# A retention stage in chunks of 64 positions, by quadrants of the matmul array

## The chip, the core and the metric

One core of a Trainium2 chip runs the whole program. Its engines have their own instruction queues, each worked off in order: TensorE (PE; its weight loads are listed as PEld), VectorE (DVE), ScalarE (ACT), GpSimd (POOL) and SyncE (SP, which issues most DMAs). The metric is the device time of one execution in microseconds (us).

## The reference

Inputs are q, k and v of 4 sequences, 8 heads, 576 positions and 64 columns a head, in fp32, and the weights of two feed-forward layers. The part that matters here is the first:

```python
scores = scale * np.matmul(q, k.transpose(0, 1, 3, 2))
Dmat = np.where(rel >= 0, gamma[:, None, None] ** rel[None, :, :], 0.0)   # rel = row - column
ret = scores * Dmat[None, :, :, :]
return np.matmul(ret, v)
```

The result, with heads side by side (2304 tokens, 512 columns), goes through `h * tanh(softplus(h))` with h = x @ w_in (2048 wide) and @ w_out, and then through a gated layer of 1536 columns and its output product.

## The kernel before, in words

The decay gamma ** (row - column) is split into a factor on v (`gv`), a factor on the result (`gout`) and a causal mask. So a sequence can be worked in chunks: inside a chunk the masked scores times v, and for all earlier positions one 64x64 state a head, the running sum of k times v.

`retention` goes through 20 steps t, five a sequence: four chunks of 128 positions and a last one of 64 (numbered sc = 0 to 4; steps 4, 9, 14 and 19 have 64). Heads are held in four pairs, a pair's two heads in the two halves of the 128 partitions. A step does, in this program order, which is the order of each engine's queue (the schedule is manual):

- `scores(t)`: for each head, keys (transposed, `kT`) against queries (`qT`), K = 64, into two PSUM tiles; then two mask multiplies on DVE into `p`, one for each half of the heads (L449).
- at steps 9, 11, 14 and 17, `g1`: the first four hidden products of the next stage (L613).
- `transposes(t + 1)`: keys of the next step through PE into `tk`, copied to `kT` by ACT; POOL makes `vs`, v times its factor.
- `q_ahead`: query transposes for later steps through the one PSUM tile `tq`, each copied by two ACT copies (L395), for the last chunk by one small copy.
- ACT and POOL split a finished weight unit into two parts (`part`, L133, L134); DVE starts on another (`begin`, L119).
- `output(t)`: the product of queries with the state, all of K = 128 against a block-diagonal `sbd` (L507); `state(t)`: k times v added to a PSUM tile (L483); `state_out`: two ACT copies of it into `sbd`, read in the next step (L497); the masked scores times v on top of the state's product (L516); and the eviction with `gout` on DVE (L529).
- the end of the step: `join` (L123), `rebias` of the next weight unit on ACT and DVE (L114, L115; the first to wait for that unit's DMA), a split of finished outputs (L318, L323), `mish` and its cast for the product of the step before (L664, L671), and the loads of later q, k, v and of a weight unit (512 KB) on SP. Steps 9, 14, 18 and 19 do no weight conversion.

fp32 matmuls go through the array in two passes, so a trace counts two a product. PSUM has eight banks: the retention uses six, `pha` two that stay for the later stages. After the retention the rest of the kernel runs: the hidden products and `acc` products in turn (L613, L647), then the same layers in a scheme of seven products for eight (L842), whose tiles alternate between the two banks of `pha`.

Of the kernel before, what the change touches and what calls it, by code (L numbers as in the profile page):

```python
# [16 lines left out]
def retention_mish_swiglu(  # L17
# [27 lines left out]
    LAG = 4  # L45
    NA = 18
# [16 lines left out]
    pha = ctx.enter_context(tc.tile_pool(name="pha", bufs=2, space=PSUM))  # L63
# [272 lines left out]
    def retention(g1, mish, g_hi, g_lo):  # L336
        with ExitStack() as c0:
# [7 lines left out]
            mask = cp.tile([128, 128], F32, tag="mask", name="mask")  # L345
            gv = cp.tile([128, nsc, H], F32, tag="gv", name="gv")
            gout = cp.tile([128, NP, nsc * 128], F32, tag="gout", name="gout")
            gstep = cp.tile([128, NP, nsc], F32, tag="gstep", name="gstep")
            sbd = cp.tile([128, NP, 128], F32, tag="sbd", name="sbd")
# [17 lines left out]
            def load(t, nm, src):  # L367
                if 0 <= t < len(steps):
                    b, sc, n = steps[t]
                    x = ld.tile([128, H, D], F32, tag=nm, name=f"{nm}{t}", bufs=4 if nm == "k" else 3)  # L370
                    nc.sync.dma_start(
                        out=x[:n], in_=src[b, :, sc * 128:sc * 128 + n, :].rearrange("h p d -> p h d")
                    )
                    qkv[nm, t] = x
# [42 lines left out]
            def transposes(t):  # L417
# [9 lines left out]
                vs[t] = at.tile([128, H, D], F32, tag="vs", name=f"vs{t}")  # L427
                nc.gpsimd.tensor_tensor(
# [5 lines left out]

            def scores(t):
                b, sc, n = steps[t]
                s = [ps1.tile([128, NP, 128], F32, tag=f"s{e}", name=f"s{e}_{t}") for e in range(2)]
                for pr in range(NP):
                    for e in range(2):
                        nc.tensor.matmul(  # L440
                            s[e][:n, pr, :n],
                            lhsT=kT[t][64 * e:64 * e + 64, pr, :n],
                            rhs=q_cols(t)[64 * e:64 * e + 64, pr],
                            start=True,
                            stop=True,
                        )
                pp[t] = [at.tile([128, NP, 128], F32, tag=f"p{e}", name=f"p{e}_{t}") for e in range(2)]
                for e in range(2):
                    nc.vector.tensor_tensor(  # L449
                        out=pp[t][e][:n, :, :n],  # L450
                        in0=s[e][:n, :, :n],
                        in1=mask[:n, :n].unsqueeze(1).to_broadcast([n, NP, n]),
                        op=ALU.mult,
                    )
# [19 lines left out]
            def state(t):  # L474
# [3 lines left out]
                if sc == 0:  # L478
                    stp[b] = ps1.tile([128, NP, D], F32, tag="st", name=f"state{b}")
                for pr in range(NP):  # L480
                    for e in range(2):
# [3 lines left out]
                            lhsT=qkv["k", t][:n, h, :],  # L485
                            rhs=vs[t][:n, h, :],
                            start=(sc == 0 and pr == 0),
                            stop=(sc == nsc - 2),
                            skip_group_check=True,
                        )  # L490

            def state_out(t):
                b, sc, n = steps[t]
                if sc == nsc - 1:
                    return
                for e in range(2):
                    nc.scalar.copy(  # L497
                        out=sbd[64 * e:64 * e + 64, :, 64 * e:64 * e + 64],
                        in_=stp[b][64 * e:64 * e + 64, :, :],
                    )  # L500

            def output(t):
                b, sc, n = steps[t]
                o = ps1.tile([128, NP, 128], F32, tag="o", name=f"o{t}")
                if sc:
                    for pr in range(NP):
                        nc.tensor.matmul(  # L507
                            o[:, pr, :n], lhsT=sbd[:, pr, :], rhs=q_cols(t)[:, pr],
                            start=(pr == 0), stop=False, skip_group_check=True,
                        )  # L510
                q_ahead(t, 1)
                state(t)
                state_out(t)
                for pr in range(NP):
                    for e in range(2):
                        nc.tensor.matmul(  # L516
                            o[64 * e:64 * e + 64, pr, :n],
                            lhsT=vs[t][:n, 2 * pr + e, :],
                            rhs=pp[t][e][:n, pr, :n],
                            start=(sc == 0 and pr == 0), stop=True, skip_group_check=True,  # L520
                        )
                t0 = b * S + sc * 128
                done = 0
                while done < n:
                    j, off = divmod(t0 + done, T)
                    m = min(n - done, T - off)
                    if j not in xt:
                        new_x(xt, j, "x")
                    nc.vector.tensor_tensor(  # L529
                        out=xt[j][:, :, off:off + m],  # L530
# [658 lines left out]
```

## Time and profile before

| | us |
|---|---|
| median of 3 runs | 916.92 (916.43 to 917.99) |
| profiled execution | 916.83 |
| its span, first to last instruction | 915.0 |
| PE busy | 904.5 |
| DVE busy | 565.7 |
| ACT busy | 378.2 |
| first product after the retention starts at | 105.67 |

The span is what the trace covers; the execution's own time is 1.8 us longer. Busy time of PE contains the time in which matmuls wait in the pipeline, so 99% does not mean that PE could do no more. The granted TensorE clock is 1.00 over the span. The stage that the change touches is the first 105.67 us.

### The profile page before, as it was taken

What the parts mean: (1) busy time and instruction counts of PE and PEld (TensorE: products, weight loads), DVE (VectorE), ACT (ScalarE), POOL (GpSimd) and SP (SyncE); (2) the same over time, 40 slices, a digit from 0 to 9 for tenths busy, and PEclk for the clock granted to TensorE, in tenths of its full rate; (3) what the DMA queues carried; (4) which work ended last, traced back from release to release, by engine and by line L of the source; (5) the groups of instructions that cost most, each with busy time, mean ns of one, the idle gap of its engine ahead of it and who ended that gap; (6) DMA issues with size and microseconds to landing.
All of it is one profiled execution on the core that took longest, in us unless ns stands there. A gap on an engine that the chain in (4) does not pass through costs nothing.

```text
span 915.0 us, 15212 instructions
## 1 busy us (share of the span) xinstructions
PE 904.5 (99%) x5828; PEld 861.5 (94%) x5828; DVE 565.7 (62%) x1094; ACT 378.2 (41%) x790; POOL 57.0 (6%) x55
## 2 busy tenths in 40 slices
PE   8999999999999999999999999999999999999998
PEld 7888999999999999999999999999999999999997
DVE  3888598467767864677664666747444556444444
ACT  3867466445555544444444333323222223222222
POOL 3654200000000000000000000000000000000000
PEclk9999999999999999999999999999999999999999
DMA  9999265257886647598737566545544444644421
GB/s 219 255 242 250 70 185 184 81 191 270 273 276 210 226 166 266 175 309 284 240 119 299 198 199 198 177 161 182 198 161 161 161 161 160 216 158 160 159 93 69
DMA packets 125016, 177.58 MB, mean 194 GB/s; under 512 B 46352, under 2 KB 83984, under 8 KB 124944
## 3 DMA queue, kind: packets, MB, share of 16 engines
q1 hardware_dynamic: 123840, 176.19, 60.9%
q8 instruction: 46, 0.75, 0.3%
q10 hardware_dynamic: 1104, 0.42, 0.2%
q14 instruction: 26, 0.21, 0.1%
HBM read 133.07 MB, written 43.52 MB: 193 GB/s over the span
## 4 chain that ended last, share of the span: by engine, by line
PE 90%; DVE 4%; DMA 2%; ACT 2%; issue 1%; SPq 0%; ACTq 0%; DVEq 0%
PE t L842 28%; PE fa L1022 16%; PE h L613 14%; PE acc L647 13%; PE ea L884 7%; PE te L842 6%; PE o L516 2%; DMA q<-in_q_dram 1%; DMA raw<-in_moe_w_out_dram 1%; PE s L440 1%; PE acc L855 1%; PE o L507 1%; DVE p L449 1%; DVE raw L123 1%; PE tk L424 0%
## 5 line engine op out<-in xcount | busy, mean ns | idle before, releaser
L842 PE MATMUL t<-y,su 128*128 128x384 f32 x1512 | 306.7, 338 | 1.1 <-ACT p L1094 0.6
L842 PEld LDWEIGHTS t<-y,su 128*128 128x128 f32 x1512 | 270.7, 188 | 24.5 <-DVE cv L849 1.8
L1022 PE MATMUL fa<-fu,g 128*128 128x512 f32 x648 | 190.2, 395 | 0.1
L613 PE MATMUL h<-xs,u 128*128 128x384 f32 x768 | 143.7, 336 | 0.0
L647 PE MATMUL acc<-g,u 128*128 128x384 f32 x720 | 134.6, 335 | 0.4 <-DVE u L134 0.4
L613 PEld LDWEIGHTS h<-xs,u 128*128 128x128 f32 x768 | 133.9, 188 | 0.4
L647 PEld LDWEIGHTS acc<-g,u 128*128 128x128 f32 x720 | 125.8, 188 | 0.7 <-DVE u L134 0.7
L1022 PEld LDWEIGHTS fa<-fu,g 128*128 128x128 f32 x648 | 118.5, 188 | 7.7 <-ACT g L1045 0.5
L1045 ACT CAST g<-sg 128x384 fp32r<-128x384 f32 x72 | 37.0, 513 | 173.3 <-DVE sg L1081 120.5
L884 PE MATMUL ea<-ge,u 128*128 128x256 f32 x576 | 77.3, 281 | 0.0
L884 PEld LDWEIGHTS ea<-ge,u 128*128 128x128 f32 x576 | 75.4, 189 | 0.0
L675 DVE TENSOR_TENSOR g<-m,g 128x384 fp32r<-128x384 f32 x64 | 36.6, 571 | 60.2 <-ACT g L671 58.8
L842 PE MATMUL te<-ye,eu 128*128 128x384 f32 x336 | 67.9, 337 | 0.0
L1070 ACT ACTIVATE sg<-sg 128x384 f32<-128x384 f32 x54 | 28.4, 526 | 91.2 <-DVE sg L849 91.2
L1050 DVE TENSOR_TENSOR g<-sg,g 128x384 fp32r<-128x384 f32 x72 | 40.2, 558 | 40.7 <-ACT g L1045 40.7
L664 ACT ACTIVATE m<-h 128x384 f32<-128x384 f32 x64 | 31.2, 488 | 66.1 <-PE h L613 66.1
L842 PEld LDWEIGHTS te<-ye,eu 128*128 128x128 f32 x336 | 56.9, 188 | 0.0
L849 DVE TENSOR_TENSOR u<-t,p 128x384 f32<-128x384 f32 x36 | 20.0, 556 | 44.3 <-PE t L842 41.1
L849 DVE TENSOR_TENSOR v<-t,p 128x384 f32<-128x384 f32 x36 | 20.0, 556 | 35.4 <-PE t L842 34.7
L671 ACT CAST g<-m 128x384 fp32r<-128x384 f32 x64 | 32.9, 514 | 1.8
L1081 DVE TENSOR_TENSOR sg<-sg,cv 128x384 f32<-128x384 f32 x54 | 30.2, 558 | 1.9
L123 DVE SCALAR_TENSOR_TENSOR raw<-raw 128x512 uint32<-128x512 uint32 x32 | 28.4, 886 | 0.0
(117 smaller groups left out, 963.7 us busy)
## 6 DMA issues: line engine op xcount, KB each, us to landing
su<-comb SPq DMA_DIRECT2D x126, 512.0 KB, 3.3
comb<-c SPq DMA_DIRECT2D x84, 256.0 KB, 2.6
eu<-ecomb SPq DMA_DIRECT2D x28, 512.0 KB, 4.9
raw<-in_moe_w_in_dram SPq DMA_DIRECT2D x16, 512.0 KB, 5.5
raw<-in_moe_w_out_dram SPq DMA_DIRECT2D x16, 512.0 KB, 3.9
ecomb<-e_s SPq DMA_DIRECT2D x32, 256.0 KB, 2.3
rawg<-in_moe_w_gate_dram SPq DMA_DIRECT2D x12, 512.0 KB, 5.6
ecomb<-u SPq DMA_DIRECT2D x24, 256.0 KB, 3.2
```

Of the source, the lines that this page charges most:

```text
L123: nc.vector.scalar_tensor_tensor(lo, hi, 3, lo, op0=ALU.logical_shift_left, op1=ALU.bitwise_or)
L613: nc.tensor.matmul(ps, lhsT=u[:, a, kk * 128:(kk + 1) * 128], rhs=s[:, e, :], start=(c == 0), stop=(c == n - 1),)
L647: nc.tensor.matmul(accs[b][d][:, :T], lhsT=u[:, a, d * 128:(d + 1) * 128], rhs=g[:, e, :], start=(i == 0 and c == 0), stop=(i == F1 - 1 an ...
L664: nc.scalar.activation(w, hs.pop(s), AF.Mish)
L671: nc.scalar.copy(out=gs[s][:, 0, :], in_=ws[s])
L675: nc.vector.tensor_tensor(out=g[:, 1, :], in0=ws.pop(s), in1=g[:, 0, :].bitcast(F32), op=ALU.subtract)
L842: nc.tensor.matmul(p, lhsT=w[:, a, kk * 128:(kk + 1) * 128], rhs=y[kk][:, x, :], start=begin and kk == 0 and (a, x) == (0, 0), stop=kk == ...
L849: nc.vector.tensor_tensor(out=out_, in0=a, in1=b_, op=ALU.add)
L884: nc.tensor.matmul(o, lhsT=u[:, a, d * 128:(d + 1) * 128], rhs=y, start=f == 0 and (a, x) == (0, 0) and (r == 0 or r == 2 and d % 2 == 0), ...
L1022: nc.tensor.matmul(accs["f", b][m], lhsT=gs[u, e, h][:, x, m * 128:(m + 1) * 128], rhs=fu[2 * (u % PAIRS) + e][:, a, :], start=first, stop ...
L1045: nc.scalar.copy(out=gs[u, e, h][:, 0, :], in_=x)
L1050: nc.vector.tensor_tensor(out=g[:, 1, :], in0=x, in1=g[:, 0, :].bitcast(F32), op=ALU.subtract)
```

## The change

Everything in the retention goes by chunks of C = 64 positions, two to a step. The scores of a step become four blocks (two chunks, two heads of a pair) in the four 64x64 quadrants of the array, into one tile `s` of two banks, with one mask multiply; the cross terms between a step's two chunks go through the state. The state is updated twice a step, each time from half of the positions, and each time ACT copies it whole into a fresh `sbd` tile (three buffers). The product with the state is done for each chunk, each head by itself on the diagonal quadrants, into two PSUM tiles `o0` and `o1`; the product with v uses four quadrants; two evictions follow. The last chunk puts the two heads of a pair into the two halves of the partitions, for which v is loaded by two DMAs and its factor `gvl` by two more.

The order of a step is new: first state update, `part`, `begin` and `join`, `mish` and its cast, product with the state, key transposes, query transposes, `g1`, second state update, scores of the next step, product with v, masks of the next step, and the end of the step as before. Query transposes and query loads come one step earlier. `pha` keeps one bank; `phb` takes another after the retention, and `front` alternates between them.

```diff
-    pha = ctx.enter_context(tc.tile_pool(name="pha", bufs=2, space=PSUM))
+    pha = ctx.enter_context(tc.tile_pool(name="pha", bufs=1, space=PSUM))
...
+                    if n == C and nm == "v":
+                        for e in range(2):
+                            nc.sync.dma_start(
+                                out=x[C * e:C * e + C, :NP, :],
+                                in_=src[b, :, sc * 128:sc * 128 + n, :].rearrange("(a e) p d -> e p a d", e=2)[e],
+                            )
+                        return
...
                 due = (
-                    ((b, 1, 0),) if b else (),
-                    ((b, 1, 1),) if b else ((b, 1, 0), (b, 1, 1)),
-                    ((b, 2, 0),),
-                    ((b + 1, 0, 0),),
+                    ((b, 1, 1),) if b else (),
+                    ((b, 2, 0),) if b else ((b, 1, 0), (b, 1, 1)),
+                    ((b + 1, 0, 0),) if b else ((b, 2, 0), (b + 1, 0, 0)),
                     ((b + 1, 0, 1),),
+                    ((b + 1, 1, 0),),
                 )[sc]
...
             def scores(t):
...
+                for pr in range(NP):
+                    for c in range(n // C):
+                        for e in range(2):
+                            nc.tensor.matmul(
+                                s[C * c:C * c + C, e, pr, :],
+                                lhsT=kT[t][64 * e:64 * e + 64, pr, C * c:C * c + C],
+                                rhs=q_cols(t)[64 * e:64 * e + 64, pr, C * c:C * c + C],
+                                start=True,
+                                stop=True,
+                            )
+
+            def masks(t):
...
+                nc.vector.tensor_tensor(
+                    out=pp[t][:, :r], in0=s[:, :r],
+                    in1=mask.unsqueeze(1).unsqueeze(1).to_broadcast([128, r, NP, C]),
+                    op=ALU.mult,
+                )
...
-            def state(t):
+            def state(t, c):
...
-                            lhsT=qkv["k", t][:n, h, :],
-                            rhs=vs[t][:n, h, :],
+                            lhsT=qkv["k", t][C * c:C * c + C, h, :],
+                            rhs=vs[t][C * c:C * c + C, h, :],
...
+                sbd[t, c] = at.tile([128, NP, D], F32, tag="sbd", name=f"sbd{t}_{c}", bufs=3)
+                nc.scalar.copy(out=sbd[t, c], in_=stp[b])
+
+            def inter(t):
...
+                                outs_[t][c][64 * e:64 * e + 64, pr, :],
+                                lhsT=sbd[(t, 0) if c else (t - 1, 1)][64 * e:64 * e + 64, pr, :],
+                                rhs=q_cols(t)[64 * e:64 * e + 64, pr, C * c:C * c + C],
...
+            def products(t):
...
+                                o[c][64 * e:64 * e + 64, pr, :],
+                                lhsT=vs[t][C * e:C * e + C, pr, :] if n == C else vs[t][C * c:C * c + C, 2 * pr + e, :],
+                                rhs=pp[t][C * e:C * e + C, 0, pr, :] if n == C else pp[t][C * c:C * c + C, e, pr, :],
...
+            for e in range(2):
+                nc.scalar.dma_start(
+                    out=gvl[C * e:C * e + C], in_=gv_d[:C, nsc - 1, :].rearrange("p (a e) -> e p a", e=2)[e]
+                )
...
+            scores(0)
+            masks(0)
             for t in range(len(steps)):
-                scores(t)
-                if t in EARLY:
-                    g1(EARLY.index(t))
-                transposes(t + 1)
-                q_ahead(t, 0)
+                state(t, 0)
                 while stage[3] < stage[2]:
                     part(NA)
                 x = due.pop(0) if due else None
                 conv = t not in REST
                 on = conv and begin()
-                if t + 1 < nsc:
-                    gout_chunk(t + 1)
-                output(t)
                 if on:
                     join(stage[2])
                     stage[2] += 1
+                if t - 1 in EARLY:
+                    mish(EARLY.index(t - 1))
+                    g_hi(EARLY.index(t - 1))
+                inter(t)
+                transposes(t + 1)
+                q_ahead(t, 0)
+                if t in EARLY:
+                    g1(EARLY.index(t))
+                state(t, 1)
+                q_ahead(t, 1)
+                if t + 1 < nsc:
+                    gout_chunk(t + 1)
+                scores(t + 1)
+                products(t)
+                masks(t + 1)
...
                 if t == 0:
                     load_q(4)
-                load_q(t + 5)
+                    load_q(5)
+                load_q(t + 6)
...
+            return front(name) if n >= LAG else pha.tile([128, T], F32, tag="h", name=name)
+
+        nfront = [0]
+
+        def front(name):
+            nfront[0] += 1
+            return (pha, pools["phb"])[nfront[0] % 2].tile([128, T], F32, tag="h", name=name)
...
+        pools["phb"] = ctx.enter_context(tc.tile_pool(name="phb", bufs=1, space=PSUM, reuse_waits="tile"))
...
-                    t[tn] = pha.tile([128, T], F32, tag="h", name=f"te{i}_{tn}")
+                    t[tn] = front(f"te{i}_{tn}")
```

## Rows read from the trace of the kernel before

**Rows 1.** The page: busy us of each engine (share of the span) and instructions.
```profile
PE 904.5 (99%) x5828; PEld 861.5 (94%) x5828; DVE 565.7 (62%) x1094; ACT 378.2 (41%) x790; POOL 57.0 (6%) x55
```

**Rows 2.** Timeline of PE, 0 to 110: start, length in us, instructions, [idle before].
```profile
15.52 0.66 PE L393 MATMUL tq<-ident,q 128*128 128x128 f32 x4 [0.80 <-DMA q<-in_q_dram]
...
17.62 0.66 PE L393 MATMUL tq<-ident,q 128*128 128x128 f32 x4 [0.55 <-DVE qT L395]
...
19.70 1.18 PE L440 MATMUL s<-qT,kT 64*128 64x128 f32 x16
...
57.07 1.27 PE L440 MATMUL s<-qT,kT 64*128 64x128 f32 x16
...
105.67 2.35 PE L613 MATMUL h<-xs,u 128*128 128x384 f32 x12
```

**Rows 3.** Windows: length; busy us (instructions) by engine; granted clock; DMA share; GB/s.
```profile
25.00:50.00 25.00, 24.16 (x338) 21.23 (x335) 23.27 (x34) 18.73 (x37) 16.51 (x14) 1.00 1.10 255
...
75.00:100.00 25.00, 24.57 (x313) 21.80 (x313) 18.45 (x29) 16.28 (x31) 11.11 (x9) 1.00 0.77 184
...
125.00:150.00 25.00, 25.00 (x146) 25.00 (x145) 22.61 (x42) 17.31 (x32) 0.00 (x0) 1.00 0.60 188
```

**Rows 4.** Timeline of PE in step 6.
```profile
37.08 1.16 PE L440 MATMUL s<-qT,kT 64*128 64x128 f32 x16
38.17 0.66 PE L424 MATMUL tk<-ident,k 128*128 128x128 f32 x4
...
39.10 1.06 PE L507 MATMUL o<-qT,sbd 128*128 128x128 f32 x8
40.09 0.69 PE L483 MATMUL state<-vs,k 128*64 128x64 f32 x16
40.60 1.05 PE L516 MATMUL o<-p,vs 128*64 128x128 f32 x16
41.58 1.16 PE L440 MATMUL s<-qT,kT 64*128 64x128 f32 x16
```

**Rows 5.** Timeline of PE in step 4, which has 64 positions.
```profile
28.67 0.68 PE L440 MATMUL s<-qT,kT 64*64 64x64 f32 x16
29.28 0.66 PE L424 MATMUL tk<-ident,k 128*128 128x128 f32 x4
```

**Rows 6.** Windows of 20 ns in a state update: PE busy (matmuls under way).
```profile
27.32:27.34 0.02, 0.02 (x4) 1.00 0.98 243
27.34:27.36 0.02, 0.02 (x6) 1.00 1.38 333
```

**Rows 7.** Groups by shape, 0 to 110: busy us, mean ns, idle before.
```profile
L449 DVE TENSOR_TENSOR p<-s,mask 128x512 f32<-128x512 f32 x32 | 20.5, 681 | 3.5 <-PE s L440 3.5
...
L529 DVE TENSOR_TENSOR x<-o,gout 128x256 f32<-128x256 f32 x8 | 3.2, 420 | 4.3 <-PE o L516 4.2
...
L664 ACT ACTIVATE m<-h 128x384 f32<-128x384 f32 x5 | 2.5, 491 | 4.4 <-PE h L613 4.4
...
L426 ACT COPY kT<-tk 128x256 f32<-128x256 f32 x4 | 1.5, 372 | 1.5 <-PE tk L424 1.3
```

**Rows 8.** Timeline of ACT in steps 5 and 6.
```profile
34.45 0.59 ACT L426 COPY kT<-tk 128x512 f32<-128x512 f32 x1
34.93 1.27 ACT L395 COPY qT<-tq 64x512 f32<-64x512 f32 x2
36.10 0.67 ACT L133 CAST u<-raw 128x512 fp32r<-128x512 f32 x1
...
38.17 0.70 ACT L114 ACTIVATE raw<-raw 128x512 f32<-128x512 f32 x1 [0.62 <-DMA raw<-in_moe_w_in_dram]
38.77 0.50 ACT L318 CAST xs<-x 128x384 fp32r<-128x384 f32 x1
```

**Rows 9.** The chain of waits in step 7: start, length, what.
```profile
42.49 6.58 DMA raw<-in_moe_w_out_dram
```

**Rows 10.** DMA queues, 0 to 110: packets, MB, share of 16 engines.
```profile
q1 hardware_dynamic: 54608, 23.07, 90.9%
```

More of the change, by code (lines that the diff above doesn't have):

```diff
@@ L433, in transposes @@
                 )
+            sc_ = {}
             def scores(t):
+                if t >= len(steps):
+                    return
                 b, sc, n = steps[t]
-                s = [ps1.tile([128, NP, 128], F32, tag=f"s{e}", name=f"s{e}_{t}") for e in range(2)]
-                for pr in range(NP):
[L439 to L454, printed above, removed]
+                s = ps1.tile([128, 2, 512], F32, tag="s", name=f"s{t}")[:, :, :NP * C]
@@ L489, in state @@
                             skip_group_check=True,
                         )
-            def state_out(t):
+                sbd[t, c] = at.tile([128, NP, D], F32, tag="sbd", name=f"sbd{t}_{c}", bufs=3)
+                nc.scalar.copy(out=sbd[t, c], in_=stp[b])
+            outs_ = {}
+            def inter(t):
                 b, sc, n = steps[t]
[L494 to L500, printed above, removed]
@@ L502, in output @@
-            def output(t):
-                b, sc, n = steps[t]
[L504 to L513, printed above, removed]
-                for pr in range(NP):
[L515 to L526, printed above, removed]
+                outs_[t] = [ps1.tile([128, NP, C], F32, tag=f"o{c}", name=f"o{t}_{c}") for c in range(n // C)]
@@ new lines, in inter @@
+                for c in range(n // C):
+                    for pr in range(NP if sc or c else 0):
+                        for e in range(2):
+                            nc.tensor.matmul(
+                                outs_[t][c][64 * e:64 * e + 64, pr, :],
+                                lhsT=sbd[(t, 0) if c else (t - 1, 1)][64 * e:64 * e + 64, pr, :],
+                                rhs=q_cols(t)[64 * e:64 * e + 64, pr, C * c:C * c + C],
+                                start=(pr == 0), stop=False, skip_group_check=True,
+                            )
@@ new lines, in products @@
+            def products(t):
+                b, sc, n = steps[t]
+                o = outs_.pop(t)
+                for pr in range(NP):
+                    for c in range(n // C):
+                        for e in range(2):
+                            nc.tensor.matmul(
+                                o[c][64 * e:64 * e + 64, pr, :],
+                                lhsT=vs[t][C * e:C * e + C, pr, :] if n == C else vs[t][C * c:C * c + C, 2 * pr + e, :],
+                                rhs=pp[t][C * e:C * e + C, 0, pr, :] if n == C else pp[t][C * c:C * c + C, e, pr, :],
+                                start=(sc == 0 and c == 0 and pr == 0), stop=True, skip_group_check=True,
+                            )
+                for c in range(n // C):
+                    j, off = divmod(b * S + sc * 128 + C * c, T)
@@ L544, in retention @@
             load(0, "v", v)
-            nc.scalar.dma_start(out=mask, in_=mask_d)
+            for c in range(2):
+                nc.scalar.dma_start(out=mask[C * c:C * c + C], in_=mask_d[C * c:C * c + C, C * c:C * c + C])
             nc.scalar.dma_start(out=gv, in_=gv_d)
@@ L548, in retention @@
             nc.scalar.dma_start(out=gstep, in_=gstep_d)
+            for e in range(2):
+                nc.scalar.dma_start(
+                    out=gvl[C * e:C * e + C], in_=gv_d[:C, nsc - 1, :].rearrange("p (a e) -> e p a", e=2)[e]
+                )
             load(1, "k", k)
```

62 lines of the change are left out of this document (42 added, 20 removed).

## The prediction

> **What bounds the kernel now.** The page's first part comes first: PE is busy 904.5 of 915.0 us [rows 1], so time can only leave where PE has less to do or waits less. The change touches only the retention, which ends where the first product of the next stage starts, at 105.67 [rows 2]. From 125 to 150 PE is busy 25.00 of 25 us [rows 3], and what is converted there hangs on PE's own progress. So I pass on one for one what the retention gains or loses.
>
> Inside the retention the windows show two limits close together [rows 3]: from 25 to 50 PE is busy 24.16, DVE 23.27 and ACT 18.73 of 25 us, with the DMA engines never empty (share 1.10); from 75 to 100 PE is as busy, but the DMA share is down to 0.77. One step in time order, step 6 [rows 4]: scores 37.08, transposes 38.17, product with the state 39.10, state update 40.09, product with v 40.60, next scores 41.58. That is 4.50 us without a gap: PE bounds the step.
>
> **The change, part by part.**
>
> Matmuls. A state update is 16 matmuls (eight fp32 products in two passes each) of 64 columns in two halves of the array; it takes 0.51 [rows 4], and such a group followed by another partition of the array takes 0.61 [rows 5]. I take 0.5 for a group and 0.1 for a change of partition. From one slice of 20 ns to the next the matmuls under way go from 4 to 6 [rows 6]: two start at once, and the halves run side by side. After the change a full step has the state update twice (each with half the rows, 0.5 + 0.6 for 0.51), the product with the state in two halves of two quadrants (1.0 for 0.99), and scores and product with v as 32 matmuls in four quadrants. No row shows four quadrants. If four run side by side, 32 matmuls take 0.5; if only two do, 1.0 (twice 0.51). I take 0.5, because halves by rows and halves by columns both pair in the rows. PE's step: 0.5 + 1.0 + 0.1 + 0.93 (transposes) + 0.6 + 0.5 + 0.5 = 4.1, against 4.50. Over 16 full steps that is 6.4 us off PE; the four steps of 64 positions use two quadrants before and after, and change by nothing.
>
> DVE. One mask multiply of 0.68 in place of two, and two evictions of 0.42 in place of one as wide as a mask multiply [rows 7]: 0.5 a step less, on an engine whose masks now have a whole step. Its remaining place on the path is an eviction ahead of the next product with the state; the 0.5 state update hides all but 0.2 of it. If that cover goes, 0.4 a step.
>
> The new wait. Before, a state copy had until the next step. Now the second half of a step's product with the state waits for ACT's copy of the state just made, and the next step's first state update writes the PSUM tile that ACT's second copy reads. ACT works in order, so whatever stands ahead of those copies is on the path. Going round from the start of the first copy: copy 0.37 [rows 7] and 0.06 for the signal, half product 0.5, change 0.1, transposes to their last result 0.66 [rows 4], so ACT's copy of the keys starts at 1.69. It takes 0.48 and the two query copies 1.17, by start to start [rows 8], so the second state copy starts at 3.34 and ends at 3.71. Then the next step's state update with its tail, 0.69 [rows 4], and a signal: 4.5. With the two ACT pieces of the conversion behind it, 0.60 and 0.50 [rows 8], ACT itself is ready only at 4.8. So PE's 4.1 is not reached in a step with two query copies: it takes 4.5 to 4.8, the 4.50 of before. Only the third step of each sequence, which has one small query copy, comes down to 4.1. Queued behind these copies on ACT: key copy, Mish, conversion; PE waits for the first, DVE for the last. The Mish of an early product and its cast (0.5 each [rows 7]) now stand ahead of the key copy, beside the transposes: 0.25 of them sticks out.
>
> Loads. Query tiles are loaded a step earlier, so 512 KB goes ahead of keys and of a weight unit in a queue that is always full: at 255 GB/s [rows 3] the unit lands 2.1 us later. Weight units already land when ACT wants them: one has 6.58 us of the chain [rows 9]. As such a wait now holds the next state copy, I put 0.7 on each of two steps. The last step's gate values come as 512 pieces of 4 bytes; a packet of the big queue costs 0.909 x 110 x 16 / 54608 = 29 ns of an engine [rows 10], so 0.9 us if a piece costs a packet, 0 if it hides; I keep 0.3. The split last v loads move the same bytes.
>
> The start. Step 1 transposes two groups of queries through one PSUM tile: the first at 15.52, after 0.80 of idle time for its DMA, the second at 17.62, after its copies, and scores 2 follow at 19.70 [rows 2]. In the new order these transposes have a state update (0.5), a product with the state (1.0) and a state copy with tail and signal (0.7) more ahead of them, and a change of partition (0.1). The idle 0.8 takes part of that; 1.5 is left, and it goes through to scores 2 at 21.2.
>
> Sum. Scores now stand at the end of the step before, so I compare the state's start after with the scores' end before: 22.3 for 20.8 at step 2, 1.5 late. Steps 2 to 9 by the lengths above (4.9 with two query groups; 4.5; 3.5 for 64 positions without a state copy; 4.6; 4.1 and 0.7; 4.7; 4.4 and 0.7; 5.6 with a product of the next stage) make 37.7; before 57.07 + 1.09 - 20.8 = 37.4: 1.8 late. Steps 10 to 19: 4.75, 6.15, 4.75, 4.5, 4.9, 4.75, 4.1, 5.9, 3.5, 1.2, together 44.5. Where a product of the next stage stands in a step I added 2.1 to 2.2 (12 such matmuls take 2.35 with their tail [rows 2]); steps with a Mish have 4.75, step 16 one small copy; step 19 has only its two products. Before: 105.67 - 57.07 - 1.09 = 47.5. So 3.0 is won there, and the retention ends at 104.5, 1.2 earlier. The profiled execution took 916.83 (span 915.0 and 1.8 around it; the runs' median is 916.92), so 915.6.
>
> **The rivals.**
>
> A. PE's saving comes through: ACT's copies are quicker in line than I put them, because Mish, conversion and query copies fall into gaps. For it: ACT is busy only 18.73 of 25 us. Against: the round is made of latencies, not of ACT's load. Then full steps of the second half take 4.1 to 4.2: its sum is 40.5, and half of the first half's lag is made good: 47.5 - 40.5 - 0.9 = 6 us, 910.8.
>
> B. Slower: ACT's wait for weight units. Place: the conversion's first ACT piece at the end of steps 4 to 8. Price: every landing that is 2.1 later, and 0.9 more for the small pieces, now holds a state copy and with it PE. It decides as soon as the units land later than the end of their step, which in the chain they already do [rows 9]. Four such steps at 1.1 instead of two at 0.7, and 0.9 at the start, bring 3.9 us more, so 919.5.
>
> C. Slower: the four quadrants go two at a time. Scores and product take 1.0 each; the round is then PE's 5.1, less the slack to 4.5: 0.6 in some 14 steps, 8 us more than my sum, so 924. Against: both kinds of halves pair. Beside it stands a sentence of the Trainium skill, "TensorE: Matmul & The Clock Gate", section "Wait — 56ns, not 53.3ns?": it says that matmuls never start closer together than about 25 ns. By that rule 32 matmuls take at least 0.8 us, 0.3 more than I put, twice a step; as an estimate from that page some 2 to 3 us on my sum. The trace does not agree: two matmuls start within one slice of 20 ns [rows 6].
>
> D. The 0.4 of an eviction ahead of the product with the state also sticks out: 16 x 0.2 = 3.2 us, which turns 915.6 into 918.8. I count it with B.
>
> **How the numbers follow.** A difference under 0.2%, 1.8 us, is about what a measurement of this kernel can tell from no change. My forecast, the round through ACT at about the length of PE's old step, has 0.50 and its own range is 913 to 918: of it 0.18 is faster, 0.30 within the bound, 0.02 slower. A has 0.18, all faster. B with D has 0.22: 0.10 within, 0.12 slower. C has 0.10, all slower. That makes 0.36 faster, 0.40 the same, 0.24 slower. The range goes from A's time to just past B's: 910.8 to 920.5; below it lies about 0.08, above it 0.12, most of that C.
>
> **What would show it.** Right: in the PE rows of steps 5 to 8 and 12 to 13, a group of 32 scores takes 0.5 to 0.6; the second half of the product with the state starts right after ACT's state copy, and the step is 4.5 to 4.8; the wait named on PE is ACT's, no longer DVE's mask. The first product of the next stage starts near 104.5. Wrong: 32 matmuls in 0.8 to 1.0 (C); steps of 4.1 with ACT idle ahead of each state copy (A); ACT's weight-unit wait over 3 us in steps 4 to 8 followed by PE (B). If the stage after the retention shows new gaps, passing the gain on one for one was wrong.

## The result, and where the time went

The changed kernel takes 924.08 us (median of 4 runs, 923.54 to 924.46); the kernel before took 917.17 in the same session (916.43 to 917.99). The ratio is 1.0075, with a 95% interval of 1.0057 to 1.0092: slower, and outside the range forecast. The profiled execution took 924.46, its span is 922.6, against 916.83 and 915.0.

The page first. Busy time of PE went down, not up, though it issues 1152 more instructions:

```profile
PE 900.7 (98%) x6980; PEld 858.3 (93%) x6980; DVE 555.7 (60%) x1088; ACT 376.5 (41%) x790; POOL 59.3 (6%) x55
```

DVE lost 10.0 and PE 3.8 us of busy time against [rows 1], and the span is 7.6 longer. So the loss is idle time of PE. The timeline of PE says where (start, length, instructions, idle time before and what ended it):

```profile
10.35 0.68 PE L523 MATMUL state<-vs,k 64*64 64x64 f32 x16 [0.66 <-POOL vs L446]
11.50 1.12 PE L542 MATMUL o<-qT,sbd 64*64 64x64 f32 x16 [0.47 <-ACT sbd L532]
...
19.98 0.66 PE L403 MATMUL tq<-ident,q 128*128 128x128 f32 x4 [0.92 <-DVE qT L405]
...
22.06 1.02 PE L476 MATMUL s<-qT,kT 64*64 64x64 f32 x27 [1.16 <-DVE qT L405]
...
23.62 0.31 PE L523 MATMUL state<-vs,k 64*64 64x64 f32 x1
...
28.20 0.69 PE L476 MATMUL s<-qT,kT 64*64 64x64 f32 x32
28.72 0.65 PE L555 MATMUL o<-p,vs 64*64 64x64 f32 x32
29.18 0.64 PE L523 MATMUL state<-vs,k 64*64 64x64 f32 x16
...
34.40 0.76 PE L542 MATMUL o<-qT,sbd 64*64 64x64 f32 x16 [0.60 <-DVE x L565]
...
39.33 0.68 PE L523 MATMUL state<-vs,k 64*64 64x64 f32 x16 [1.70 <-POOL vs L446]
40.54 0.68 PE L542 MATMUL o<-qT,sbd 64*64 64x64 f32 x16 [0.53 <-ACT sbd L532]
...
44.33 0.59 PE L523 MATMUL state<-vs,k 64*64 64x64 f32 x13 [0.54 <-ACT sbd L532]
...
65.09 0.27 PE L523 MATMUL state<-vs,k 64*64 64x64 f32 x1
...
113.26 2.37 PE L660 MATMUL h<-xs,u 128*128 128x384 f32 x12
```

Read it in three parts. The last line answers to 105.67 in [rows 2]: the retention ends 7.59 later, and the span is longer by 7.6, so the rest of the kernel carries that one for one. The three lines at 28 to 29 us show the quadrants doing what was hoped: 32 scores in 0.52, 32 products in 0.46 (start to start), where 16 matmuls in two halves took 0.98 to 1.09 [rows 4]. And the brackets from 34 to 45 us, two steps, name DVE, POOL and twice ACT: it is not one engine that is late. (23.62 and 65.09 are the first state updates of steps 2 and 10; they are used below.)

The windows give the account (length; busy us of PE, PEld, DVE, ACT, POOL; granted clock; DMA share; GB/s). First the kernel before, from 8 us to the end of its retention, then the changed one in the same bounds, in a stretch that answers to [rows 3], and in two short ones:

```profile
8.00:105.67 97.67, 94.06 (x1234) 82.81 (x1233) 74.98 (x109) 64.23 (x124) 50.62 (x43) 1.00 0.98 227
```

```profile
8.00:113.26 105.26, 89.77 (x2376) 79.14 (x2374) 64.09 (x102) 61.12 (x124) 53.13 (x43) 0.97 0.91 212
...
25.00:50.00 25.00, 20.59 (x587) 17.75 (x587) 17.00 (x27) 17.26 (x35) 15.66 (x14) 1.00 1.06 247
...
11.50:15.00 3.50, 3.50 (x58) 3.05 (x62) 0.00 (x0) 0.82 (x2) 2.05 (x2) 0.51 1.26 258
21.80:25.20 3.40, 3.14 (x88) 3.15 (x90) 1.27 (x4) 0.23 (x1) 0.98 (x1) 0.50 1.17 269
```

Idle time is length less busy time: 97.67 - 94.06 = 3.6 before, 105.26 - 89.77 = 15.5 after. The two short stretches ran at half clock (0.51 and 0.50, that is 1.2 GHz); of their 6.6 us of work half, 3.3, would not have been there at 2.4 GHz. The profiled execution before has no such stretch. So TensorE's work, counted at full clock, fell from 94.1 to 89.77 - 3.3 = 86.5 us, and the balance is -7.6 of work, +11.9 of idle time, +3.3 of half clock: +7.6.

Who ended the idle time stands in the waits view (engine, line, waited for: us in total, times, longest). Before:

```profile
PE o L516 <- DVE p L449: 1.7, 7, 0.6
PE tq L393 <- DMA q<-in_q_dram: 0.8, 1, 0.8
PE tq L393 <- DVE qT L395: 0.6, 1, 0.6
PE o L507 <- DVE x L529: 0.3, 1, 0.3
```

After:

```profile
PE o L542 <- DVE x L565: 2.7, 4, 1.0
PE state L523 <- POOL vs L446: 2.7, 3, 1.7
PE o L542 <- ACT sbd L532: 2.1, 4, 0.5
PE state L523 <- ACT sbd L532: 1.9, 4, 0.5
PE s L476 <- DVE qT L405: 1.2, 1, 1.2
PE tk L434 <- DMA k<-in_k_dram: 0.9, 1, 0.9
PE tq L403 <- DVE qT L405: 0.9, 1, 0.9
PE s L476 <- ACT kT L436: 0.9, 2, 0.6
PE state L523 <- issue: 0.8, 2, 0.6
PE o L555 <- issue: 0.6, 1, 0.6
```

No row holds a fifth of the 15.5. The mask, the one regular wait before, is gone; ten others came.

### The profile page after: what moved, and what is told of

It is laid out like the page before. It is cut to its first block, busy times and chain, and to the rows that moved or that the text cites. A ratio compares the mean times of both kernels' runs of the same rounds, so it can differ in the third digit from the quotient of the medians.

```text
span 922.6 us, 17529 instructions
## 1 busy us (share of the span) xinstructions
PE 900.7 (98%) x6980; PEld 858.3 (93%) x6980; DVE 555.7 (60%) x1088; ACT 376.5 (41%) x790; POOL 59.3 (6%) x55
## 4 chain that ended last, share of the span: by engine, by line
PE 90%; DVE 3%; ACT 2%; DMA 2%; POOL 1%; issue 1%; SPq 0%; ACTq 0%; POOLq 0%; DVEq 0%
PE t L898 28%; PE fa L1078 16%; PE h L660 14%; PE acc L702 13%; PE ea L940 7%; PE te L898 6%; PE o L542 1%; PE state L523 1%; DMA v<-in_v_dram 1%; PE acc L911 1%; PE tk L434 1%; PE o L555 1%; PE s L476 1%; PE tq L403 1%; DVE raw L120 1%
## 5 line engine op out<-in xcount | busy, mean ns | idle before, releaser
L730 DVE TENSOR_TENSOR g<-m,g 128x384 fp32r<-128x384 f32 x64 | 35.8, 559 | 55.5 <-ACT g L726 55.3
L565 DVE TENSOR_TENSOR x<-o,gout 128x256 f32<-128x256 f32 x36 | 13.8, 419 | 34.8 <-PE o L555 34.8
```

The lines of the kernel that those rows point to most:

```text
L730: nc.vector.tensor_tensor(out=g[:, 1, :], in0=ws.pop(s), in1=g[:, 0, :].bitcast(F32), op=ALU.subtract)
```

## The experiments

The theory at the start: the loss is a sum of single waits in the new round, above all ACT's two state copies, and each comes back when its cause is taken away. Its rival: another wait is found behind each. All times beside the runs are from their profiled executions, by the account above (end of the retention; idle time of PE from 8 us on; work at half clock; work of PE counted at full clock). Ratios are to the kernel before on the same chip.

| run | median us | ratio (95%) | end | idle | at half clock | work |
|---|---|---|---|---|---|---|
| before | 917.17 | | 105.67 | 3.6 | 0 | 94.1 |
| after | 924.08 | 1.0075 (1.0057 to 1.0092) | 113.26 | 15.5 | 6.6 | 86.5 |
| e1, new order with chunks of 128 | 933.96 | 1.0188 (1.0162 to 1.0214) | 124.75 | 17.5 | 8.9 | 94.8 |
| e2, 40 fillers | 928.04 | 1.0125 (1.0101 to 1.0149) | 117.20 | 10.9 | 3.4 | 96.6 |
| e3, no wait for the copy inside a step | 923.49 | 1.0073 (1.0057 to 1.0090) | 114.11 | 15.0 | 10.2 | 86.0 |
| e5, POOL's values first | 924.46 | 1.0083 (1.0058 to 1.0108) | 111.70 | 14.7 | 6.7 | 85.6 |
| e6, state product later in end steps | 923.33 | 1.0072 (1.0055 to 1.0090) | 115.00 | 14.6 | 10.2 | 87.3 |
| e7, second update earlier | 926.30 | 1.0105 (1.0087 to 1.0124) | 115.60 | 13.8 | 6.8 | 90.4 |
| e8, 15 fillers | 926.30 | 1.0093 (1.0076 to 1.0109) | 114.57 | 13.3 | 3.2 | 91.7 |
| e9, another bank for the queries | 926.05 | 1.0097 (1.0081 to 1.0113) | 116.10 | 15.8 | 12.9 | 85.9 |
| e10, second copy on DVE | 923.88 | 1.0079 (1.0064 to 1.0095) | 114.13 | 13.9 | 13.1 | 85.7 |
| e12, e5, e6, e10 and five key buffers | 927.52 | 1.0116 (1.0100 to 1.0133) | 116.16 | 13.6 | 17.0 | 86.0 |
| e11, before with split matmuls | 928.08 | 1.0122 (1.0107 to 1.0137) | 117.13 | 1.6 | 6.8 | 104.2 |
| x1, before with quadrant scores | 916.61 | 0.9993 (0.9984 to 1.0002) | 105.98 | 4.5 | 0 | 93.5 |
| x2, x1 and quadrant state product | 918.56 | 1.0018 (1.0008 to 1.0027) | 106.95 | 5.2 | 0 | 93.8 |
| y1, before with less of the product | 915.51 | 0.9986 (0.9977 to 0.9995) | 103.40 | 4.3 | 0 | 91.1 |

### Order or chunks (e1)

The chunking is undone, and the order, the query schedule and the loads of the change stay. The one state update of a step stands where the changed kernel has its second. Part of the edit, against the kernel before:

```diff
-                output(t)
...
+                inter(t)
+                transposes(t + 1)
+                q_ahead(t, 0)
...
+                state(t)
+                state_out(t)
+                q_ahead(t, 1)
...
+                scores(t + 1)
+                products(t)
+                masks(t + 1)
```

> Chunks of 128 positions as before, with the changed kernel's order of steps, its query schedule and its loads: only the chunking is undone. One state update and one state copy a step, scores and product as 16 matmuls in two halves. Theory 'chunks' (the second state copy a step and the half product that waits for it cost the time, and the new order is harmless): between 915 and 918, steps 10 to 19 in about 47. Rival 'order' (two query groups transposed late in step 1, scores at the end of the step, loads one step earlier cost it): 922 or more, with the second step's state update again near 23 us instead of near 20.8.

Measured: 933.96, worse than the change itself. Two steps of its PE timeline:

```profile
58.43 1.09 PE L529 MATMUL o<-p,vs 128*64 128x128 f32 x16
60.41 1.13 PE L519 MATMUL o<-qT,sbd 128*128 128x128 f32 x8 [0.89 <-DVE x L542]
...
63.67 1.09 PE L529 MATMUL o<-p,vs 128*64 128x128 f32 x16
65.65 0.52 PE L519 MATMUL o<-qT,sbd 128*128 128x64 f32 x3 [0.89 <-DVE x L542]
```

With scores at the end of a step, the product with v is followed at once by the next product with the state, which needs the same PSUM tile evicted: 0.86 to 0.95 in fourteen of the twenty steps, 12.6 us in all. The waits view up to 120 us has thirteen of them:

```profile
PE o L519 <- DVE x L542: 11.7, 13, 1.0
```

So this order without the chunks loses 17 us, and the chunks win 10 of them back. Part of that is that their first state update lies over the eviction, whose row is 2.7 in the changed kernel. The rival had the direction, and scores at the end of the step among its reasons, but not this wait. The run shows that the order costs much where nothing covers the eviction. It does not show that the order is the loss of the changed kernel, where this wait is mostly covered. The fourth kernel, chunks of 64 in the old order, was not tried.

### One wait at a time (e3, e5, e6, e7, e9, e10)

```diff
 # e3, inter(): the second half reads the copy of the step before
-lhsT=sbd[(t, 0) if c else (t - 1, 1)]...
+lhsT=sbd[(t - 1, 1) if sc else (t, 0)]...
 # e5, POOL's subtract of part() moved behind vs of the next step
                 while stage[3] < stage[2]:
-                    part(NA)
+                    part_hi()
...
                 transposes(t + 1)
+                part_lo()
...
 # e6: last step, product behind transposes and queries; first step, behind queries
-                inter(t)
+                if sc == 0:
+                    q_ahead(t, 0)
+                if sc < nsc - 1:
+                    inter(t)
                 transposes(t + 1)
-                q_ahead(t, 0)
+                if sc:
+                    q_ahead(t, 0)
+                if sc == nsc - 1:
+                    inter(t)
 # e7
                 transposes(t + 1)
+                state(t, 1)
                 q_ahead(t, 0)
...
-                state(t, 1)
 # e9, second query group of step 1
-q_transposes(*due[half])
+q_transposes(*due[half], *(("tk",) if t == 1 and half else ()))
 # e10
-nc.scalar.copy(out=sbd[t, c], in_=stp[b])
+(nc.vector.tensor_copy if c else nc.scalar.copy)(out=sbd[t, c], in_=stp[b])
```

> The changed kernel, but the second half of the product with the state reads the state copy of the step before (where there is one), so that it no longer waits for the copy made in this step; the copy itself stays. The contribution of the first 64 positions of a step to its second 64 is left out. Theory 'round' (ACT's state copy in the middle of the step sets its length): the waits of 0.25 to 0.75 us ahead of the second half go, full steps fall from 5.0 to about 4.5, and the time to 917 to 919. Rival 'other waits' (POOL's values, the evictions, the loads and the start cost it, and the step finds its slack elsewhere): 922 or more.

> The changed kernel, but POOL makes the next step's scaled values before it makes the low part of the weight unit (ACT's high part stays where it is). TensorE sat idle 2.7 us for POOL's values up to the end of the retention (1.7 of it at 37.6 us). Theory 'waits of each kind' (the loss is a sum of single waits, each of which comes back when its cause goes): those waits go, about 2.5 us less, 921.5. Rival 'next wait' (what is taken away is found again at the next engine): no change, 923.5 to 924.5.

> The changed kernel, but in the last step of each sequence the key and query transposes stand ahead of the product with the state, and in the first step the first query group does. TensorE sat idle 0.5 to 1.0 us ahead of that product in each of the four last steps, for the eviction of the step before (no state update covers it there), and 0.53 in three first steps, for the state copy. Theory 'waits of each kind': 2.7 plus 1.6 go, about 4 us less, 920. Rival 'next wait' (the product of the last step, now later, is late for the scores or evictions that follow): less than 1 us.

> The changed kernel with the second state update of a step ahead of its first query group instead of behind it, so that ACT copies the state before the query group and not after. Theory 'round': the waits of about 0.7 us for the state copy ahead of the next step's first state update go in the six to eight steps that have them, so 3 to 5 us less: 919 to 921. Rival: the query copies come as much later, and the second query group or the next scores wait for them instead: 924, or up to 2 us more.

> The changed kernel, but the second query group of step 1 is transposed through the PSUM bank of the key tile, so that it waits for ACT's key copy (0.6 us) and not for the two query copies; nothing else. TensorE sat idle 0.92 ahead of that group and 1.16 behind it. Theory 'waits of each kind': the 0.92 goes, and with it a cause of the half clock from 21.8 on; 1 to 2.5 us less: 921.5 to 923. Rival: ACT and DVE copy in order and the second group's copies end as late as before, so the scores of step 2 do too: 923.5 to 924.5.

> The changed kernel, but DVE makes the second state copy of a step, in place of ACT, where it stands behind two query copies. Four waits of about 0.5 us ahead of the next step's first update (43.8, 69.6, 80.9, 95.9) and some of 0.1 to 0.2 come from there. Theory 'round': they go, 2 to 3 us less, 921 to 922. Rival 'next wait': DVE's copy of 0.4 stands ahead of the evictions, which make the next product late; 923.5 to 925.

Measured: none is faster than the changed kernel beyond its interval; e7 and e9 are some 2 us slower, and e9's 926.05 lies outside both of its forecasts. The wait aimed at did go where its row could be followed. In e5 POOL's rows fell from 2.7 to 0.4, and this is what its waits view then has:

```profile
PE tk L434 <- DMA k<-in_k_dram: 2.0, 1, 2.0
...
PE state L542 <- issue: 1.5, 1, 1.5
...
PE o L574 <- issue: 0.7, 1, 0.7
PE state L542 <- POOL vs L446: 0.4, 1, 0.4
```

The key load's wait grew from 0.9 to 2.0 and the two issue rows from 1.4 to 2.2. In e6 the row of DVE's eviction fell from 2.7 to 0.6 and that of ACT's state copy from 2.1 to 0.5, but POOL's values went from 2.7 to 4.3 and ACT's key copy from 0.9 to 2.5; in e10 ACT's second copy (1.9) became DVE's (2.6). That is the rival's picture: the idle time stays at 13.8 to 15.8 whichever wait is taken away. It is not the whole of it in e5: its profiled execution, with about the same time at half clock as the changed kernel's (6.7 and 6.6), ended the retention 1.6 us earlier and took 923.34 for 924.46. Some 1 us may have come back there; the spread of e5's five runs (921.35 to 927.50) is too wide to tell. e3 missed: its theory put 0.25 to 0.75 on every full step. But the four long waits of that row (2.1 us, 0.5 each) stand in the first step of each sequence, where e3 keeps them, as there is no earlier copy to read; in the other steps the copy was hardly waited for, and taking that away gave 0.6 us in the median and nothing in the ratio. e7 shows a price of its own, 3.9 us more work of PE, the update standing between two groups of transposes; the cause stays open.

### All at once (e12)

> The changed kernel with several cures at once: POOL's values ahead of the unit's low part, the product with the state of a first or last step behind transposes, the second state copy on DVE, and five key buffers in place of four. Each alone left the time at 923 to 926, as others came in its place. Theory 'waits are parallel' (a step has several waits of nearly one length, so one alone gives nothing, all together give most of their 8 us): 917 to 919, idle time of TensorE up to the end of the retention from 15.5 to 8. Rival 'fetch and clock' (what is left is the fetching of instructions and the stretches at half clock that any idling brings): 921 to 923, with issue gaps of 2 us or more and two or three stretches of 3.4 us at half clock.

Idle time fell only to 13.6 (ACT's key copy 4.1 and DVE's state copy 2.9 lead its list, both moved there by the edits), so the waits are not simply parallel. And 17 us of its retention ran at half clock:

```profile
11.90:15.30 3.40, 3.40 (x82) 3.07 (x83) 0.42 (x1) 0.58 (x1) 1.80 (x2) 0.50 1.26 260
22.10:25.50 3.40, 3.40 (x100) 3.40 (x92) 1.35 (x3) 0.37 (x1) 1.72 (x2) 0.50 1.10 267
46.00:52.80 6.80, 6.80 (x137) 6.24 (x138) 4.47 (x8) 2.94 (x7) 3.71 (x3) 0.50 1.02 259
87.00:90.40 3.40, 3.40 (x55) 2.95 (x53) 1.70 (x5) 1.13 (x2) 1.79 (x2) 0.50 1.15 277
```

TensorE is busy through all of these rows, so by the account above half of the 17 is lost in this execution: 8.5 us, more than the cures could bring. How much of it reaches the time is not shown: of the four runs the one with the lowest mean clock, 0.989, was the fastest (926.83), and one at 0.992 the slowest (928.27). The rival had this right in kind (half clock, and issue gaps of 1.9 us in all) and too low in time.

### The clock (e2, e8)

```diff
+            fill(7)                         # e8: 2
             scores(0)
+            fill(6)                         # e8: 2
...
                 state(t, 0)
+                if t == 0:
+                    fill(6)                 # e8: 2
...
                 state(t, 1)
+                if t == 1:
+                    fill(9)                 # e8: 4
                 q_ahead(t, 1)
+                if t == 1:
+                    fill(12)                # e8: 5
```

> The changed kernel with some 40 matmuls on zeros put into the idle gaps of TensorE in steps 0 and 1 (ahead of scores 0, after them, after the first state update, after the second update of step 1 and after its second query group), to keep the engine busy there; nothing else. Theory 'clock' (the two stretches at half clock, 11.5 to 15.0 and 21.8 to 25.2 us, come from those gaps and cost the time that their work takes double): both stretches at full clock, the state update of step 2 at about 21 instead of 23.6, and 921 to 921.5. Rival 'waits' (TensorE waits for ACT and DVE there anyway, so its clock costs nothing): 924, or more by what the fillers delay.

> The changed kernel with fillers at the same places as in the first trial, but 15 in place of 40 (a filler is two passes of 0.109 us, so 0.22: some 3.3 us in all against the 3.8 us that TensorE is idle there, each group no longer than its gap). Theory 'clock': full clock up to 25 us, scores at the same times as in the changed kernel or earlier, and 2 to 3 us less: 921 to 922. Rival: the half-clock stretch comes later instead, at the next idle gaps (in the first trial one of 3.4 us at 44.4), and the time is within 1 us of 924.

Both keep the granted clock at 1.00 up to 25 us. Both get a half-clock stretch later instead (44.4 to 47.8, and 51.1 to 54.5), at an idle gap, as the rival of e8 has it. Its time it has not: the fillers cost more than they save, 4.0 and 2.2 us on the changed kernel's 924.08. What the clock costs shows better among runs of one kernel: e5's took 921.35 at a mean clock of 1.000, 923.34 at 0.996 and 924.46 to 927.50 at 0.994; e1's 932.0 and 932.1 at 1.000, 935.8 and 936.3 at 0.995. In others it is less: e10's took 923.22 at 1.000 and 923.84 at 0.996, e11's 927.34 at 1.000 and 928.03 to 928.25 at 0.996. The changed kernel has no run at 1.000; its runs took 923.54 at 0.998 and 923.83 and 924.46 at 0.996. So the half clock is an estimated 0.6 to 4 of the 7 us, by these differences,, and a run without it is still slower than the kernel before. That kernel is not free of it in every run either: some of its runs without a trace have a mean clock of 0.998.

### Instructions (e11), and quadrants in the old order (x1, x2)

```diff
 # e11: scores and product of the kernel before, each matmul as two of 64 columns
+                    for z in range(0, n, 64):
...
-rhs=q_cols(t)[64 * e:64 * e + 64, pr],
+rhs=q_cols(t)[64 * e:64 * e + 64, pr, z:z + 64],
...
 # x1: scores in quadrants
+                    for c in range(0, n, 64):
...
-s[e][:n, pr, :n], lhsT=kT[t][64 * e:64 * e + 64, pr, :n],
+s[e][c:c + 64, pr, :n], lhsT=kT[t][64 * e:64 * e + 64, pr, c:c + 64],
...
 # x2: and the product with the state on the diagonal
-o[:, pr, :n], lhsT=sbd[:, pr, :], rhs=q_cols(t)[:, pr],
+o[64 * e:64 * e + 64, pr, :n], lhsT=sbd[64 * e:64 * e + 64, pr, :], rhs=q_cols(t)[64 * e:64 * e + 64, pr],
```

> The kernel before (its own order, chunks of 128), but the 16 matmuls of the scores and the 16 of the product with v are each issued as two of 64 columns: the same columns, some 600 more matmuls on TensorE up to the end of the retention (about 1950 in place of 1304; the changed kernel has 2390). Theory 'fetch': the idle time that ends by nothing but issue (0 in the two kernels with chunks of 128, 1.4 to 3.6 us in every kernel with chunks of 64) follows the number of instructions: here 0.5 to 2 us of it, each gap ending 2.3 to 3.0 us after a block of 16 KB of instructions begins to arrive, and 917.5 to 920. Rival (these gaps belong to quadrant groups or to the new order): no such gap, and 916 to 918.

> The kernel before, chunks of 128 and its own order, with the scores alone as 64x64 quadrant matmuls (16 of 128 columns in four quadrants in place of 8 in two halves; all four quadrants of a chunk are computed). No new wait. A group of scores should take about 0.5 in place of 1.0 us, 8 us of TensorE's work in 16 full steps. Theory 'forced order' (the quadrants pay, the second update, copy and eviction and their order lose it): 911 to 914, idle time of TensorE up to the end of the retention 6 to 9 in place of 3.6. Rival 'nobody follows' (DVE with 23.3 of 25 us, or the half clock after new idle time, eats it): 915.5 to 918.

> As x1, and the product with the state as diagonal 64x64 quadrants of 128 columns from a state copy that is no longer block-diagonal (one ACT copy in place of two; in the last step of a sequence the product with v runs over 128 rows, the lower 64 of them against zeros, with 128 KB more loaded). Two halves took 1.0 us in the changed kernel; one pass of 128 columns on both diagonals should take 0.5 to 0.6 in place of 0.99. Theory 'forced order': 1 to 3 us below x1. Rival 'nobody follows': equal to x1 or up to 3 us slower, DVE's evictions and masks being what TensorE waits for.

e11 missed both ways: no issue gap, and nearly 12 us slower, mostly because 32 scores of half the columns take 2.00 us where 16 took 1.16 [rows 4]:

```profile
47.58 2.00 PE L441 MATMUL s<-qT,kT 64*128 64x64 f32 x32
```
Its work is 104.2, and as PE was slower there and not faster, it says nothing on fetching. It issued 512 matmuls more, not the 600 of its forecast. x1 and x2 missed on size. PE timeline of x1:

```profile
36.44 1.10 PE L441 MATMUL s<-qT,kT 64*64 64x128 f32 x32
37.47 0.66 PE L424 MATMUL tk<-ident,k 128*128 128x128 f32 x4
```

32 matmuls of 128 columns in four quadrants take 1.03 from start to start, where the 16 in two halves took 1.09 [rows 4]; x2's 16 on the diagonal take 1.02, where 0.5 to 0.6 was forecast. A quadrant moves its columns at 1 us per 1024 (8 matmuls of 128) in x1, and at 0.5 per 512 (8 of 64) in the changed kernel. So the quadrant form itself gains nothing; what halves the time in the change is that the blocks between a step's two chunks are not computed. x1 is level with the kernel before; no run with the whole computation in it was faster than that kernel.

### Can the others follow a shorter step? (y1)

```diff
-rhs=pp[t][e][:n, pr, :n],
+rhs=pp[t][e][:n, pr, :n if sc == 0 else 64],
```

> The kernel before, but in the twelve full steps that are not the first of their sequence the product with v is made for the first 64 positions alone (the other 64 get the product with the state only): that part of the result is left out. It takes about 0.5 us per step off TensorE, 6 us in all (the changed kernel saves 7.6), in the old order, with no wait, copy or eviction more. Theory 'forced order': most of it arrives, retention end near 101 and 911 to 913, TensorE's idle time up to there 3.6 to 6, no half clock. Rival 'nobody follows' (DVE's masks and evictions, POOL's values and the loads set the step at 4.5 anyway): idle time 8 or more, 915 to 917, and if idling brings the half clock, such stretches here too.

Between the two: idle time 4.3 and no half clock, as the forced order has it, but only 1.5 us faster (ratio 0.9986, 0.9977 to 0.9995). In the waits view the mask's row grew from 1.7 to 2.6:

```profile
PE o L516 <- DVE p L449: 2.6, 10, 0.4
```

So in the old order a shorter step of PE arrives for the most part (3.0 us less work, 2.3 at the end of the retention), and it costs little idle time. For 3.0 us, then, the other engines can follow; whether they could for the 7.6 of the change no run shows. It makes it likely that the loss is what the change adds: the new order, with its second copy and its second eviction.

## Why the prediction was wrong

What held. The rest of the kernel passes the retention's end on one for one (7.59 and 7.6). The four quadrants run side by side (0.52 and 0.46; I took 0.5), which refutes rival C: its time, 924, came by chance, for another reason. The floor of 25 ns between starts that the Trainium skill states ("TensorE: Matmul & The Clock Gate", section "Wait — 56ns, not 53.3ns?") would, as an estimate, make 0.8 us of 32 matmuls; this trace, with 0.46 to 0.52, does not agree. PE's work fell by 7.6 us, where I had 6.4. DVE's work fell. Rival B's mechanism did not appear: ACT waits for no weight unit in the changed retention, its piece of 14 units having no idle time before it:

```profile
L115 ACT ACTIVATE raw<-raw 128x512 f32<-128x512 f32 x14 | 9.6, 684 | 0.0
```

What failed is the step under "The new wait": I took the length of a step as the longer of PE's round (4.1) and ACT's (4.5 to 4.8), with every other engine on time, and summed such steps to 37.7 and 44.5. Measured by the start of the state updates, steps 2 to 9 took 41.5 (23.62 to 65.09) and steps 10 to 19 took 48.2 (to 113.26). Step by step the largest misses are step 4 (3.5 forecast, 4.93 measured, 1.99 of it idle), step 13 (4.5 and 5.51, 0.99 idle), step 16 (4.1 and 5.03, 0.64 idle) and step 18 (3.5 and 4.77, 0.76 idle); step 9 went the other way (5.6 and 4.59). The waits of that round are there, but they are 4.0 of 15.5 us of idle time (ACT's copy before the second half and before the next update), and e3 shows that in the ordinary steps the copy in the middle sets nothing. In its place the runs showed a loop in which each engine is late in some step:

- "3.5 for 64 positions without a state copy": these steps have no state update either, so nothing covers the eviction ahead of them: 0.60 at 34.40, 2.7 in all. I had priced that cover, 0.4 a step if it goes, and overlooked that it goes in every fifth step.
- POOL is absent from my sum. It makes the next values behind the low part of a weight unit and a split, and the next state update now comes at the start of a step: 1.70 at 39.33, 2.7 in all.
- The start: 1.5 late forecast, 2.8 measured (first update of step 2 at 23.62 for 20.8). The copies of the two query groups are the place I named (0.92 and 1.16 of idle time), with a half-clock stretch on either side.
- The half clock, 3.3 us, was in no step of mine; the clock of 1.00 before was taken as given.
- The idle time that ends by nothing but issue, 1.4 us, likewise.
- PE's 4.1 was a little short, though the saving was not. Steps 7, 8, 12, 13 and 16 kept TensorE busy for 4.4 to 4.5 us each (the last matmuls ahead of a wait counted to their end). The same five took 4.75 to 5.14 of busy time in the kernel before, where step 6 with its 4.50 was one of the short ones, so about 0.4 a step was saved.

Two slips in the sum: the step with the one small query copy is the second of the sequences after the first (6, 11 and 16), as the sum has it for 6 and 16, and not the third, as the sentence says; and steps 9 and 14, which do the same work, stand in it with 5.6 and 4.9 (4.59 and 4.60 measured).

The time at half clock is shown by rows, and its price is bounded by runs of one kernel at different clocks; the issue gaps are shown by rows alone. That waits replace each other, at least in large part, is shown by e5, e6 and e10. Why the idle total stays near 14 whichever wait goes is open. What is not settled either is how the 11.9 us of idle time divide between the order and the second copy and eviction: with chunks of 128 the order alone has more idle time (17.5) than the change.

## What to carry to other kernels

When the busiest engine's work shrinks, ask of every step what covers each of its waits, the odd steps first, and sum by the engine that is late in that step, not by the two longest rounds; a step that fits to 0.3 us has five engines that can each be late. Count the new hand-overs against the gain: in y1, which adds none, 2.3 of 3.0 us arrived, and in the change 7.6 us of work bought ten waits and nothing arrived. And once such a wait is named, taking it away alone proves little in either direction; look at the idle total.

## What the runs showed of the hardware

The half clock. In the profiles of the changed kernel and of e1 to e12 TensorE fell to 1.2 GHz in one to four stretches of the retention, in those of the kernel before, x1, x2 and y1 in none. They begin in or close behind idle gaps (0.92 and 1.16 around 21.8; 1.95 at 42.9 ahead of 46.0 in e12), none of them longer than 2.12 us. But such gaps alone do not bring it on: x2 had one of 1.01 us and the kernel before one of 0.80, without a stretch, while in e11 TensorE was busy 10.25 of the 10.8 us ahead of a stretch from 35.8 on, with a single gap of 0.55. So what brings it on stays open.

Instructions. A trace lists blocks of 16 KB on a DMA queue of their own (blocks, MB, share of the 16 engines); first the kernel before, then the changed one, up to 113 us:

```profile
q8 instruction: 10, 0.16, 0.6%
```

```profile
q8 instruction: 19, 0.31, 1.2%
```

2376 matmuls and 2374 weight loads make 250 records for each of 19 blocks. Of the ten profiles with chunks of 64 positions eight have gaps of over 0.5 us that end by nothing but issue, 16 in all, and each of the 16 ends 2.2 to 3.0 us after a block began to arrive; with chunks of 128 there is none. The Trainium skill, "Runtime: NRT & Kernel Launch", section "Instruction fetch mechanics", gives the blocks the same size, 256 instructions, and calls the cost of crossing from one to the next mostly hidden. The size agrees with this trace. If the gaps are the fetch, it is not hidden here, where 64 matmul and load instructions run off in 0.5 us; that they are is argued from their times, not shown by a run.
